# Two loads moved to ScalarE's queue, a read-back moved ahead of x, and two weight conversions regrouped in the start of a fused SSD and PReLU kernel

## The chip, the cores and the metric

The kernel runs on one core of one Trainium2 chip. The metric is the device time of one execution, in microseconds (us); lower is better. One core has a tensor engine (PE, matmuls; PEld is its weight load), VectorE (DVE), ScalarE (ACT), GpSimd (POOL) and SyncE (SP). Loads and stores are issued by SP or ACT into their own queues and carried out by 16 DMA engines.

## The reference

Two blocks follow each other. The first is a state-space scan over 4 batches, 8 heads, 768 tokens, with 32 values of x and 16 values of B and C per head and token, and one decay `a` per head and token. In chunks:

```
y_intra = (C B^T * decay between the two tokens, causal) x
y_inter = (C state) * product of the decays since the chunk began
state   = product of the chunk's decays * state + sum of B x * decays to the chunk's end
```

The second takes the result as 3072 tokens of 256 values and computes `h = x @ w_in` (256 to 2048), `g = max(h, 0) + alpha * min(h, 0)` with one alpha per column, and `out = g @ w_out` (2048 to 256). `w_in` and `w_out` arrive as float64 (8 bytes a value), everything else as float32.

## The kernel before

**Tiles and stages.** A chunk is Q = 128 tokens; two chunks are a pair (`gp`, 12 in all), two pairs are a group of 512 tokens (6 in all). For each pair the kernel loads B, C (into the tile `nat`), x (`xt`) and decays, scans, and writes the result turned into `xT` (`xts[g]`), from which the hidden matmuls read. The first group is special. `first_two` (L821) makes pairs 0 and 1 with decays spread by PE from a short form, in half chunks of 64 tokens; during it the first weights arrive and are converted. After it, group 0 goes through `hidden` and `output` one column block `f` of 128 at a time (loop at L1454), while pairs 2 and 3 are made beside it; from group 1 on `quad` does the weight products.

**Weights.** `w_in` and `w_out` come in eight pieces each (`in_pieces`, `out_pieces`), 512 KB as doubles. Their order in `pieces` (L1413) is in 0, in 1, in 2, out 0, in 3, out 1, in 4, out 2 and so on. `load_weights` (L252) puts one into a tile `raw` (six buffers) through SP. The conversion to float32 has these steps:
- `convert_a` (L262): ACT makes the magnitude of the high word (L273, `wt`); POOL, or DVE where `by` says so, clamps it (L278); ACT makes the low part (L283 or L286, `wg`).
- `sign` (L291): DVE takes the sign bit (L296, `wr`).
- `convert_b` (L300): DVE shifts and xors (L308).
- `convert` (L312): POOL adds both parts into `w_in` or `w_out` (L330).

`convert_next` (L1423) does the last step of the next piece in order, may begin another, and loads one when six are on their way.

**What sets the order.** The order of the instructions on each engine is written out by hand: each engine and each queue runs its instructions in the order in which the program gives them, and waits where data isn't there. So all that follows is read from the text of `first_two`:
- clamps and first scans; `spread` (L858), PE's products that fill the decay banks; `rows_short` (L488), which stores a short form of the products to DRAM (`short`, L500); `rows_out` (L472), a store of `z`;
- `load_pair(1)` (L170): on SP B, C, B, C (L192), x, x (L197); then `load_second` (L228), which reads `short` back, spread over partitions, into the tile `ap` of pair 1 (L231). a of pair 1 (`a1`) has been loaded in `load_pair(0)` by SP (L209, through L133);
- pair 0: `scan` (L870), `turned` (L837, transposes and copies of B and C), `spread_c` (L851), `gram_of` (L874), `added` (L890, the states' increments), `times` (L886), `states` (L903), `mask` (L914, through `one_at_a_time`);
- `first_a` (L539), which clamps `a1` on DVE into `z1`, and the loads of piece 2, of the first half of pair 2 and of piece 3;
- the conversion of piece 0 (L1013, L1014, L1022), around pair 0's `x_products` (L922), `state_products` (L935) and `spread` for pair 1; `copy_out` (L945), four ACT copies into `xT`;
- `hidden_two` (L1102) for columns 0 and 1 of pair 0's tokens; the scans of pair 1 with the conversion of piece 1 between them (L1029 to L1037); pair 1's `turned`, `added`, `states`;
- `rows_products` (L439, a scan on DVE, L441), then on SP the second B and C of pair 2, piece 4, `rows_sent` (L445, its store `pf`), x, piece 5, `abc` (L160, decays spread from `z`), `ap` of pair 2 (L168, which reads `pf` back), `abc`, pieces 6 and 7;
- `hidden_two` for columns 2 and 3, with pair 1's `gram_of`, `times`, last state, `x_products`, `state_products` and `copy_out` placed among its matmuls by `among`; then piece 2 and the rest.

`keep_warm` (L335) puts matmuls without a use where PE would stand.

Of the kernel before, what the change touches and what calls it, by code (L numbers as in the profile page):

```python
# [22 lines left out]
def kernel(  # L23
# [32 lines left out]
    P = 128  # L56
# [113 lines left out]
    def load_pair(gp, decays=True, parted=False):  # L170


        b, c = divmod(2 * gp, CPB)
        turned = gp > GC
        nat = ldx.tile([P, 3, 2, H * N], F32, name="nat")
        xt = ldx.tile([P, 2, HD], F32, name="xt")

        ap = ldx.tile([P, 2 * Q], F32, name="ap")
        if gp == 0:
            load_a(ap, b, c)  # L180
        elif gp > NB:
            load_products(gp, ap)
        if gp == 0:
            load_rows(0, nc.scalar)
        abc = []
        if gp >= HALF:
            load_tokens(nat[:, 0], B[b], c * Q)
        def load_bc(k):
            ts = slice((c + k) * Q, (c + k + 1) * Q)
            for i, src in enumerate((B,) if turned else (B, C)):  # L190
                eng = nc.scalar if gp == 0 and i else nc.sync
                eng.dma_start(out=nat[:, i, k].rearrange("p (h n) -> p h n", h=H),  # L192
                              in_=src[b, :, ts, :].rearrange("h p n -> p h n"))

        def load_x(k):
            ts = slice((c + k) * Q, (c + k + 1) * Q)
            nc.sync.dma_start(out=xt[:, k].rearrange("p (h d) -> p h d", h=H),  # L197
                              in_=x[b, :, ts, :].rearrange("h p d -> p h d"))

        for k in range((1 if parted else 2) if gp < HALF else 0):  # L200
            load_bc(k)
            if gp >= NB:
                load_x(k)
        for k in range(2 if gp < NB else 0):
            load_x(k)
        if gp == 0:
            nc.scalar.dma_start(out=al_n, in_=moe_alpha.rearrange("(k p) -> k p", p=P))
            loads["a", 1] = prep.tile([P, 2 * Q], F32, name="a1")
            load_a(loads["a", 1], b, c + 2)  # L209
        for i, src in enumerate((B, C) if turned else ()):  # L210
# [12 lines left out]
        if decays:  # L223
            for part in load_spread(gp, b, c):
                pass
        return lambda: load_bc(1), lambda: load_x(1)

    def load_second():  # L228

        rows = scratch["short", 0].rearrange("(b h c) t -> b h (c t)", b=2, h=H)  # L230
        nc.sync.dma_start(out=loads["p", 1][3], in_=rows[0, :, 2 * Q : 4 * Q].unsqueeze(1)  # L231
                          .to_broadcast([H, N, 2 * Q]))

    al_n = const.tile([NF, P], F32, name="al_n")
    load_pair(0)
# [22 lines left out]
        raws[id(dst)] = raw  # L258

    parts = {}  # L260

    def convert_a(dst, src, sg, by=nc.gpsimd):  # L262

# [557 lines left out]
    def first_two():  # L821
# [157 lines left out]
        spread(z0, sp)  # L979
        prq = rows_short(rq)  # L980
        rows_out(0)
        load_pair(1)
        load_second()
        nat1, _, xt1, pf1 = loads["p", 1]
        for r in range(4):
            scan(0, r, sp[r])
# [5 lines left out]
        nc.tensor.transpose(al_p[:, :NF], al_n, ident[:NF, :NF])  # L992
        keep_warm(al_p[:, Q:], 1, 3 * Q)
        nc.scalar.copy(out=alpha, in_=al_p[:, :NF])
        bn0 = pair_loads(0)
        slopes(alpha)
        gram_of(bc0, cz0, sp)
# [2 lines left out]
        nc.vector.tensor_tensor_scan(out=pf0, data0=z0.rearrange("p k t -> p (k t)"),  # L1000
                                     data1=starts_a, initial=0.0, op0=ALU.mult, op1=ALU.add)
        cd0 = decayed_c(bc0, pf0)
        for r in (0, 1):
            times(0, r, sp[r])
        states(0, dps, pf0)
        one_at_a_time(0, range(3))
        for r in (2, 3):
            times(0, r, sp[r])
        z1 = first_a(loads["a", 1], nc.vector, lent[1][:, 2:])
        load_next()  # L1010
        load_bc, load_x = load_pair(2, False, True)
        load_next()
        convert_a(*pieces[0], by=nc.vector)  # L1013
        convert_b(*pieces[0], ways=2)  # L1014
        y = places([ss(), ss()], [hp, tp])
        x_products(y, xt0, 0, (0,))
        sp = [bank(r) for r in range(4)]
# [1 line left out]
        x_products(y, xt0, 0, (1,))  # L1019
        state_products(y, 0, cd0)  # L1020
        spread(z1, sp)
        convert_next(halves=(nc.gpsimd, nc.gpsimd))  # L1022
        xts[0] = xtp.tile([P, KC, GT], F32, name="xT")
        copy_out(0, y)
        prelu_of = {0: hidden_two(0, 0, 0, spare())}
        keep_warm(sp[3][:, 2 * Q :], 1)


        scan(1, 0, sp[0])  # L1029
        convert_a(*pieces[1])  # L1030
# [27 lines left out]
        next(spread_loads)  # L1058
        load_next(2)
        keep_warm(second, 1)  # L1060

        def among(i, k):
# [357 lines left out]
            load_weights(*p)  # L1420
        loaded[0] += n

    def convert_next(first=True, **kw):  # L1423


        i = done[0]
        if i < len(pieces):
            convert(*pieces[i], **kw)
# [151 lines left out]
```

## Time and profile before

| | |
|---|---|
| median of 3 runs | 356.28 us (356.27 to 356.45) |
| span of the profiled execution | 355.9 us (355.92) |
| its own whole time | not given by the page; the median less the span is 0.36 us |
| PE busy | 349.3 us, 98% of the span, 2985 matmuls |
| DVE, ACT, POOL busy | 235.8, 171.8, 204.4 us |
| idle time of PE between matmuls | 3.2 us, all before 46 us |
| granted clock of PE | full in all slices |
| DMA | 30.24 MB, 105581 packets, 79896 of them under 512 B |

The profile is that of one execution. Its page gives, for each engine, how long it was busy; a busy PE includes the matmuls that only keep it warm. The timeline lists an engine's instructions in order: start, length, line, operation, output<-inputs, shape, count, and in brackets the idle time before it with what ended it. SPq and ACTq are the issues of loads; their length is the time that the issue held the queue, not the time to landing. The chain of waits goes back from the last instruction to what released it each time. Views by stretch of time give each engine's busy time there, PE's clock, the share in which the DMA engines were busy, and GB/s.

### The profile page before, as it was taken

To read this page: it belongs to the slowest core of one execution; us is meant where nothing else is said; L and a number is where in the kernel's file an instruction comes from. 1 tells how busy PE (TensorE), PEld (TensorE's weight loads), DVE (VectorE), ACT (ScalarE), POOL (GpSimd) and SP (SyncE) were. 2 spreads that over 40 slices of the span, in tenths; PEclk is the share of its full clock that TensorE was granted. 3 is DMA by queue.
4 is the path that set the end of the run, shared out by engine and by line. 5 is a ranking of instruction groups with operands and counts; after the bars stand their busy time and mean duration, and the time that the engine had idled before them with its cause. 6 is when DMAs were issued, how large, how long until landed. Compare 5 with 4: busy or idle time off the path is not lost.

```text
span 355.9 us, 7778 instructions
## 1 busy us (share of the span) xinstructions
PE 349.3 (98%) x2985; PEld 284.4 (80%) x2985; DVE 235.8 (66%) x482; ACT 171.8 (48%) x391; POOL 204.4 (57%) x228
## 2 busy tenths in 40 slices
PE   8899999999999999999999999999999999999996
PEld 4576665578788888888888888888888888888885
DVE  6876986998748756847747856757856633643363
ACT  3477576535355346345345445345445344443431
POOL 6776568589939855725646626637526535434520
PEclk9999999999999999999999999999999999999999
DMA  7899989607345403503423423422001001001102
GB/s 138 182 202 270 329 174 279 148 17 159 106 83 128 102 3 75 104 2 77 78 57 74 86 51 71 85 55 65 11 2 31 0 2 29 2 1 31 31 0 59
DMA packets 105581, 30.24 MB, mean 85 GB/s; under 512 B 79896, under 2 KB 101448, under 8 KB 105544
## 3 DMA queue, kind: packets, MB, share of 16 engines
q1 hardware_dynamic: 103048, 29.43, 36.3%
q10 hardware_dynamic: 2496, 0.32, 0.6%
q8 instruction: 23, 0.38, 0.5%
q14 instruction: 14, 0.11, 0.1%
HBM read 26.32 MB, written 3.42 MB: 84 GB/s over the span
## 4 chain that ended last, share of the span: by engine, by line
PE 89%; SPq 4%; DMA 3%; DVE 2%; ACT 1%; POOL 1%; issue 0%; DVEq 0%; ACTq 0%
PE bank L1216 33%; PE hp L1241 29%; PE bank L1142 6%; PE ss L1241 6%; PE hp L1095 3%; DMA raw<-in_moe_w_in_dram 2%; SPq L192 2%; PE ss L787 1%; PE ss L731 1%; PE hp L1110 1%; PE bank L1209 1%; PE ss L805 1%; PE ss L779 1%; DMA xt<-in_x_dram 1%; SPq L197 1%; PE ss L742 1%
## 5 line engine op out<-in xcount | busy, mean ns | idle before, releaser
L1298 POOL TENSOR_TENSOR gt<-gt 128x512 f32<-128x512 f32 x58 | 74.2, 1279 | 21.1 <-DVE gt L1226 16.3
L1216 PE MATMUL bank<-gt,w_out 128*128 128x256 f32 x320 | 83.5, 381 | 0.0
L1216 PEld LDWEIGHTS bank<-gt,w_out 128*128 128x128 f32 x320 | 60.1, 190 | 9.2 <-issue 1.0
L1288 POOL TENSOR_TENSOR gt<-gt 128x512 f32<-128x512 f32 x20 | 25.4, 1269 | 62.5 <-DVE gt L1226 49.7
L1226 DVE SCALAR_TENSOR_TENSOR gt<-hp,s_mul,gt 128x256 f32<-128x256 f32 x96 | 42.0, 479 | 29.1 <-ACT gt L1224 26.8
L1224 ACT ACTIVATE gt<-hp,s_alpha 128x256 f32<-128x256 f32 x96 | 40.3, 471 | 34.5 <-PE hp L1241 31.4
L1216 PE MATMUL bank<-gt,ws 128*128 128x256 f32 x224 | 55.9, 379 | 0.0
L1216 PEld LDWEIGHTS bank<-gt,ws 128*128 128x128 f32 x224 | 42.3, 190 | 5.6
L1241 PE MATMUL hp<-xs,w_in 128*128 128x256 f32 x160 | 41.9, 384 | 0.0
L1241 PE MATMUL hp<-xs,ws 128*128 128x256 f32 x160 | 41.1, 380 | 0.0
L1267 DVE TENSOR_TENSOR hp<-hp,u 128x512 f32<-128x512 f32 x20 | 14.0, 700 | 35.2 <-ACT u L1265 35.2
L1241 PEld LDWEIGHTS hp<-xs,ws 128*128 128x128 f32 x160 | 30.3, 190 | 4.3 <-POOL xs L1183 0.2
L1241 PEld LDWEIGHTS hp<-xs,w_in 128*128 128x128 f32 x160 | 29.7, 190 | 4.5
L1142 PE MATMUL bank<-w_out,gt 128*128 128x256 f32 x128 | 31.1, 385 | 0.4 <-POOL w_out L330 0.4
L1142 PEld LDWEIGHTS bank<-w_out,gt 128*128 128x128 f32 x128 | 23.6, 190 | 7.2 <-issue 2.9
L1241 PE MATMUL ss<-xT,w_in 128*128 128x256 f32 x96 | 24.6, 379 | 0.0
L645 POOL TENSOR_TENSOR sm<-state,bmask 128x256 f32<-128x256 f32 (+1 forms) x10 | 6.2, 620 | 29.0 <-DVE state L642 29.0
L1095 PE MATMUL hp<-xT,w_in 128*128 128x512 f32 x48 | 22.8, 596 | 0.0
L561 DVE TENSOR_TENSOR_SCAN dec<-abc,bank 128x192 f32<-128x192 f32 x48 | 22.7, 522 | 0.0
L1256 ACT COPY m<-hp 128x512 f32<-128x512 f32 x8 | 4.7, 586 | 35.7 <-PE hp L1241 35.7
L1265 ACT COPY u<-hp 128x512 f32<-128x512 f32 x20 | 11.7, 585 | 19.4 <-PE hp L1241 19.4
L1226 DVE SCALAR_TENSOR_TENSOR gt<-c,s_mul,gt 128x256 f32<-128x256 f32 x40 | 20.6, 555 | 0.0
(232 smaller groups left out, 608.2 us busy)
## 6 DMA issues: line engine op xcount, KB each, us to landing
abc<-z SPq DMA_DIRECT2D x24, 192.0 KB
raw<-in_moe_w_in_dram SPq DMA_DIRECT2D x8, 512.0 KB
raw<-in_moe_w_out_dram SPq DMA_DIRECT2D x8, 512.0 KB
abc<-z SPq DMA_DIRECT2D x8, 512.0 KB
out_dram<-o_sb SPq DMA_DIRECT2D x32, 64.0 KB
nat<-in_B_dram SPq DMA_DIRECT2D x26, 64.0 KB
xt<-in_x_dram SPq DMA_DIRECT2D x12, 128.0 KB
xt<-in_x_dram SPq DMA_DIRECT2D x24, 64.0 KB
```

The source lines that it names most:

```text
L192: eng.dma_start(out=nat[:, i, k].rearrange("p (h n) -> p h n", h=H), in_=src[b, :, ts, :].rearrange("h p n -> p h n"))
L561: nc.vector.tensor_tensor_scan(out=dv[:, o : o + SQ], data0=abc[k][:, s : s + SQ], data1=ident_p[0][:, :SQ], initial=0.0, op0=ALU.mult, op ...
L1095: nc.tensor.matmul(hp, w_in[:, k, f * P : (f + 1) * P], xts[g][:, k], start=(k == 0), stop=(k == KC - 1))
L1142: nc.tensor.matmul(pos[0][t // 2][:, t % 2], gt[:, t * Q : (t + 1) * Q], w_out[:, f], start=(f == 0 and t % 2 == 0), stop=(f == NF - 1), s ...
L1216: nc.tensor.matmul(ms[g][i][:, h], w, blocks[g, z][n][:, p], start=(q == 0 and h == 0), stop=(q == NQ - 1), skip_group_check=True)
L1224: nc.scalar.mul(o[:, p], h[:, p], s_alpha[:, fs[p]])
L1226: nc.vector.scalar_tensor_tensor(out=o[:, p], in0=h[:, p], scalar=s_mul[:, fs[p]], in1=o[:, p], op0=ALU.mult, op1=ALU.max)
L1241: nc.tensor.matmul(to[:, p], w(2 * z + p), b, start=start and p == 0, stop=True, skip_group_check=True)
L1265: nc.scalar.copy(out=u2, in_=A)
L1267: nc.vector.tensor_tensor(out=Y, in0=Y, in1=u2, op=ALU.add)
L1288: nc.gpsimd.tensor_tensor(out=tc_, in0=g22, in1=g12, op=ALU.subtract)
L1298: eng.tensor_tensor(out=o, in0=x0, in1=x1, op=ALU.subtract)
```

## The change

- `load_pair`: for pair 1 C is no longer loaded with B. A new `load_c`, on ACT's queue, loads it; `first_two` calls it twice behind the copy of alpha (L994).
- `a1` is loaded through ACT's queue, behind alpha's load.
- The read-back of `short` into `ap` of pair 1 stands in `load_pair`, after B and ahead of x; `load_second` is gone.
- `first_a` for pair 1 stands ahead of pair 0's first `times`.
- Piece 0 is converted by a new `convert_first`, after `spread` of pair 1: ACT's magnitude and low part by halves, sign whole, DVE's clamp and xor by halves, then `copy_out`, then ACT's second low part, then POOL's two adds.
- Piece 1 is clamped by DVE instead of POOL, and its whole conversion on DVE stands between the first and the second scan of pair 1.
- `rows_products`, its store and the loads behind it stand after the second `hidden_two` with its `among`, ahead of piece 2's second step; the second B and C of pair 2 and piece 4 stay where they were.

```diff
-            for i, src in enumerate((B,) if turned else (B, C)):
+            for i, src in enumerate((B,) if turned or gp == 1 else (B, C)):
...
+        def load_c(k):
+            ts = slice((c + k) * Q, (c + k + 1) * Q)
+            nc.scalar.dma_start(out=nat[:, 1, k].rearrange("p (h n) -> p h n", h=H),
+                                in_=C[b, :, ts, :].rearrange("h p n -> p h n"))
...
+        if gp == 1:
+            rows = scratch["short", 0].rearrange("(b h c) t -> b h (c t)", b=2, h=H)
+            nc.sync.dma_start(out=ap, in_=rows[0, :, 2 * Q : 4 * Q].unsqueeze(1)
+                              .to_broadcast([H, N, 2 * Q]))
         for k in range(2 if gp < NB else 0):
             load_x(k)
...
-            load_a(loads["a", 1], b, c + 2)
+            load_a(loads["a", 1], b, c + 2, nc.scalar)
...
-        return lambda: load_bc(1), lambda: load_x(1)
-
-    def load_second():
...
+        return lambda: load_bc(1), lambda: load_x(1), load_c
...
+    def convert_first(dst, src, sg, copies):
...
+        def magnitude(k):
+            nc.scalar.activation(out=t[:, k].bitcast(F32), in_=hi[:, k].bitcast(F32),
+                                 func=ACTF.Abs, scale=0.125)
+
+        def low(k):
+            nc.scalar.activation(out=g[:, k], in_=half[:, k], func=ACTF.Copy,
+                                 scale=2.0**-11, bias=2.0**25)
+
+        magnitude(0)
+        low(0)
+        magnitude(1)
+        nc.vector.tensor_single_scalar(out=r, in_=hi, scalar=SIGN, op=ALU.bitwise_and)
+        for k in range(2):
+            tk = t[:, k]
+            nc.vector.tensor_scalar(out=tk.bitcast(F32), in0=tk.bitcast(F32), scalar1=F64_INF,
+                                    scalar2=F64_ZERO, op0=ALU.min, op1=ALU.max)
+            nc.vector.scalar_tensor_tensor(out=r[:, k], in0=tk, scalar=3, in1=r[:, k],
+                                           op0=ALU.logical_shift_left, op1=ALU.bitwise_xor)
+        copies()
+        low(1)
+        for k in range(2):
+            nc.gpsimd.tensor_tensor(out=d[:, k], in0=r[:, k], in1=g.bitcast(U32)[:, k], op=ALU.add)
...
-        load_pair(1)
-        load_second()
+        load_c = load_pair(1)[2]
...
         nc.scalar.copy(out=alpha, in_=al_p[:, :NF])
+        for k in range(2):
+            load_c(k)
         bn0 = pair_loads(0)
...
         cd0 = decayed_c(bc0, pf0)
+        z1 = first_a(loads["a", 1], nc.vector, lent[1][:, 2:])
         for r in (0, 1):
             times(0, r, sp[r])
...
-        z1 = first_a(loads["a", 1], nc.vector, lent[1][:, 2:])
...
-        convert_a(*pieces[0], by=nc.vector)
-        convert_b(*pieces[0], ways=2)
...
         spread(z1, sp)
-        convert_next(halves=(nc.gpsimd, nc.gpsimd))
         xts[0] = xtp.tile([P, KC, GT], F32, name="xT")
-        copy_out(0, y)
+        convert_first(*pieces[0], lambda: copy_out(0, y))
+        convert_next(first=False, ready=moe_w_in.dtype != F32)
...
         scan(1, 0, sp[0])
-        convert_a(*pieces[1])
-        sign(*pieces[1])
-        scan(1, 1, sp[1])
+        convert_a(*pieces[1], by=nc.vector)
         convert_b(*pieces[1])
-        for r in (2, 3):
+        for r in (1, 2, 3):
             scan(1, r, sp[r])
...
-        rpf = rows_products()
         load_bc()
         load_next()
-        rows_sent(rpf)
-        load_x()
-        load_next()
-        spread_loads = load_spread(2, *divmod(4, CPB))
-        next(spread_loads)
-        load_products(NB, loads["p", NB][3])
-        next(spread_loads)
-        load_next(2)
         keep_warm(second, 1)
...
         prelu_of[2] = hidden_two(0, 2, 0, second, among)
+        rows_sent(rows_products())
+        load_x()
+        load_next()
+        spread_loads = load_spread(2, *divmod(4, CPB))
+        next(spread_loads)
+        load_products(NB, loads["p", NB][3])
+        next(spread_loads)
+        load_next(2)
```

With `ready=True`, `convert_next` only counts the piece as done and doesn't convert it.

More of the change, by code (lines that the diff above doesn't have):

```diff
@@ L225, in load_pair @@
                 pass
-        return lambda: load_bc(1), lambda: load_x(1)
-    def load_second():
-        rows = scratch["short", 0].rearrange("(b h c) t -> b h (c t)", b=2, h=H)
-        nc.sync.dma_start(out=loads["p", 1][3], in_=rows[0, :, 2 * Q : 4 * Q].unsqueeze(1)
-                          .to_broadcast([H, N, 2 * Q]))
+        return lambda: load_bc(1), lambda: load_x(1), load_c
     al_n = const.tile([NF, P], F32, name="al_n")
@@ L260 @@
     parts = {}
+    def convert_first(dst, src, sg, copies):
+        if src.dtype == F32:
+            copies()
+            return
+        d = dst.bitcast(U32)
+        raw = raws.pop(id(dst))
+        hi = raw[:, :, :, 1]
+        half = raw.rearrange("p k w t -> p k (w t)").bitcast(U16)
+        half = half.rearrange("p k (w t) -> p k w t", t=4)[:, :, :, 1]
+        t = wtp.tile([P, 2, WQ], U32, name="wt")
+        g = wtp.tile([P, 2, WQ], F32, name="wg")
+        r = wtp.tile([P, 2, WQ], U32, name="wr")
+        def magnitude(k):
[14 more added lines that the diff above has]
+                                           op0=ALU.logical_shift_left, op1=ALU.bitwise_xor)
+        copies()
+        low(1)
+        for k in range(2):
+            nc.gpsimd.tensor_tensor(out=d[:, k], in0=r[:, k], in1=g.bitcast(U32)[:, k], op=ALU.add)
     def convert_a(dst, src, sg, by=nc.gpsimd):
@@ L1008, in first_two @@
             times(0, r, sp[r])
-        z1 = first_a(loads["a", 1], nc.vector, lent[1][:, 2:])
         load_next()
-        load_bc, load_x = load_pair(2, False, True)
+        load_bc, load_x, _ = load_pair(2, False, True)
         load_next()
-        convert_a(*pieces[0], by=nc.vector)
-        convert_b(*pieces[0], ways=2)
         y = places([ss(), ss()], [hp, tp])
@@ L1421, in load_next, with convert_next @@
         loaded[0] += n
-    def convert_next(first=True, **kw):
+    def convert_next(first=True, ready=False, **kw):
         i = done[0]
         if i < len(pieces):
-            convert(*pieces[i], **kw)
+            if not ready:
+                convert(*pieces[i], **kw)
             if first and i and i + 2 < len(pieces):
```

## The prediction

> **What bounds the kernel now.** I read the page first: PE is busy for 349.3 of the 355.9 us and holds 89% of the chain of work that ended last, so time can be won only where PE stands still. The chain of waits over the first 60 us shows where that is: everything before 46 us is the start, and after it the chain is PE alone.
>
> ```profile
> 9.40 3.52 SPq L192
> ...
> 29.84 7.45 DMA raw<-in_moe_w_in_dram
> ...
> 40.34 2.33 DVE dec L567 x4
> ...
> 44.52 1.28 POOL w_out L330
> ...
> 45.84 1.99 PE bank L1142 x8
> ```
>
> Columns: start, length, what. A DMA issue that SP could not finish for 3.52 us; a weight piece that took 7.45 us from issue to landing; DVE's scans; POOL's last step of a w_out piece; then output(4) on PE. Behind that line no stall of PE over 0.03 us follows, so a shift of the start survives to the end only if the work released at 45.84 shifts too. Second, PE's timeline with its idle times (the other gaps: 0.53 at 8.27, 0.27 at 21.81):
>
> ```profile
> 14.11 2.04 PE L1110 MATMUL hp<-xT,w_in 128*128 128x256 f32 x8 [0.85 <-POOL w_in L330]
> ...
> 17.54 0.35 PE L895 MATMUL ss<-xt,bn 64*32 64x64 f32 x16 [0.25 <-DMA xt<-in_x_dram]
> ...
> 45.84 0.48 PE L1142 MATMUL bank<-w_out,gt 128*128 128x256 f32 x1 [0.44 <-POOL w_out L330]
> ```
>
> The first hidden matmuls wait for the converted first piece, `added` waits for x of pair 1, output(4) for out_pieces[2]. Third, DVE around pair 1:
>
> ```profile
> 18.30 0.98 DVE L910 SCALAR_TENSOR_TENSOR gt<-gt,ap,ss 128x64 f32<-128x64 f32 x3 [0.72 <-DMA ap<-short]
> 19.20 0.83 DVE L441 TENSOR_TENSOR_SCAN rpf<-r,zeros 96x128 f32<-96x128 f32 x1
> 20.08 1.42 DVE L887 TENSOR_TENSOR dec<-bank,dec 128x256 f32<-128x256 f32 x4
> ```
>
> `states` waits for the products `ap`, then `rows_products` (0.83 us) stands between it and `times`, which x_products on PE needs. Fourth, SP's queue, and the DMA engines (last two columns: busy share, GB/s):
>
> ```profile
> 9.40 3.52 SPq L192 DMA_DIRECT2D nat<-in_B_dram  x1
> 12.96 0.58 SPq L192 DMA_DIRECT2D nat<-in_C_dram  x1
> 13.59 1.21 SPq L197 DMA_DIRECT2D xt<-in_x_dram  x2
> 14.84 0.67 SPq L231 DMA_DIRECT2D ap<-short  x1
> ```
> ```profile
> 12.00:13.50 1.50, 1.25 (x44) 0.94 (x42) 1.22 (x4) 1.50 (x7) 0.22 (x1) 1.00 0.24 28
> ...
> 38.00:42.00 4.00, 4.00 (x27) 2.30 (x26) 3.50 (x7) 4.00 (x9) 2.71 (x3) 1.00 1.05 403
> ```
>
> SP hangs in B's second issue until 12.92 while the DMA engines run dry (share 0.24); from 30 to 42 they are full (0.99 to 1.05).
>
> **The change, part by part.** All starts are those of the profile before.
>
> *a of pair 1 on ScalarE's queue.* SP loses 0.65 + 0.05 us, so the weights are issued at 5.10, not 5.80. ACT gains one issue of 0.65 to 0.80 (rows L133): its table load (1.28, at 3.69) ends at 5.77 at the latest, and its first copy starts at 5.79, so it is hidden with 0.02 to spare; past that, bc, cz and alpha (8.11) follow one for one. The bytes still go through the same engines (share 0.87 from 6 to 8), beside x and B of pair 0. Landing of the first piece (11.54): between 0.7 earlier and 0.3 later; I take 0 to 0.2 earlier, since the engines were nearly full.
>
> *C of pair 1 on ScalarE's queue.* Two issues behind the alpha copy (ends 8.28). Nearest row: ACT's own C issues, 1.30 for two; ACT is taken until 9.6, and its next work is the L906 copy at 9.51: cost 0 to 0.1, covered by PE's two warm matmuls (10.14 to 11.27). Queued behind: L906, then the first piece's conversion.
>
> *z1 earlier on DVE.* 0.28 + 0.06, into the 0.40 that DVE waits for L881 before `times` (8.97). Free if a1 has landed by 8.6; it was not waited for at 11.26, so its landing isn't bounded by a row here; taken as free.
>
> *First piece by halves.* Now ACT L273 0.67, L283 0.66, then four copies, DVE clamp 0.43 and two 0.38, POOL two 0.85; PE at 14.11. Half-size ACT steps: bounds 0.37 (L847 copy) and 0.57 (half of L286 x2); I take 0.42 (L1120, also 128x256). From 11.54: magnitudes and low part end at 11.96, 12.31, 12.66; DVE clamps a half in 0.28 (L437, 128x252) and xors in 0.38: 12.62 and 13.36; POOL follows 0.16 later (23.60 to 23.76): first half ready at 13.63, 0.48 earlier. The second half waits for ACT: copies to 13.40, low(1) to 13.78, POOL to 14.75, against 14.97. So the four matmul pairs end 0.2 to 0.5 earlier; I take 0.35. With 0.57 per ACT step it is 0.
>
> *Second piece.* Its clamp leaves POOL (0.61 at 15.05) for DVE (0.43), ahead of scans 1 to 3 (1.9 together); the 0.72 that DVE waited for that clamp goes. Scans end near 17.35 instead of 17.57, POOL's bn1 and the piece itself come 0.9 earlier.
>
> *Products ahead of x, no C between.* On SP: short and z stores, B, B, then `ap`, which reads back the short store, x, x, next weight piece. B's second issue no longer stalls behind a full queue, but SP now waits for the short store to land. The trace's landing events put that at 13.05 (the last of its completions). Then `ap` 0.1 + 0.67, x from 13.86 (13.59 before), the next piece from 15.1 (15.55). x now meets empty engines instead of C's 1024 packets of 64 B, so it lands at 16.6 to 17.7 against 17.50; I take 17.1. `ap` lands near 15.5 against 18.2, and L910's 0.72 wait goes; next late are the scans.
>
> *rows_products moved.* Times start when L881 is done (19.2) instead of 20.08; x_products ends 1.1 earlier, and with 0.2 of issue left over PE enters the L1110 run at 22.3 instead of 23.2: **0.9 ahead**. Its new place is after L296 (22.81): 0.83 more before L308 and POOL's 1.40 of piece 2 (ends 25.16, needed 27.28): hidden by 2.1 - 0.83. Its store waited for nothing at 24.15 on SP; with the scan done at 23.64 at the latest there is 0.5 of cover. Without it, pf, `ap` of pair 2 (which already waits 0.9 for pf) and all weights behind slip one for one. x, out_pieces[1], two abc, `ap` and two more pieces move with it, in the same SP order.
>
> *What is late next.* PE comes to output(4) 0.9 sooner, but that needs in_pieces[4] landed (37.29) and, from there to 45.8, DVE without a pause over 0.5. Those landings follow SP's stream through full engines. The stream gains between 0 (same bytes) and 1.1 us (1.5 us at share 0.24 refilled); the read-back of short leaves 0.45 at the next weight piece, and I take 0.5 to 0.6. PE's wait at 45.84 then grows from 0.44 to about 0.8 and swallows the rest.
>
> The Trainium skill (DMA: Bandwidth & Descriptors, Issuing engines are not separate DMA queues) says that loads started by different engines share the same 16 DMA engines, so that only issue time is saved. The trace agrees: 3178 packets in 1.5 us with two queues (2119 per us), 1096 in 0.5 us with one (2192). By the rule alone the stream gains 1.9 us of issue at most; by the rows the engines are the limit and it gains the 0.5.
>
> **Sum.** Span 355.92 - 0.55 = 355.37. The page gives no whole time; the median 356.28 stands 0.36 above the span, taken as unchanged: **355.7**.
>
> **Rivals.**
> 1. *The stream gains its 1.1 us or more.* For it: share 0.24 and the 3.52 us. Against: the wait for short. Then PE's 0.9 and most of the 0.44 count: 1.0 to 1.4, so 354.9 to 355.3.
> 2. *Hidden anyway.* Landings at 32.5 and 37.3 unchanged, because the engines are full; PE is early and waits 1.3 at 45.84, or the halves gain nothing since the second still ends near 14.97. Time 356.1 to 356.5.
> 3. *Slower: ScalarE is held by its own loads.* At 37.30 SP waited 0.7 for a weight piece that this load of B or C doesn't touch; the trace has it waiting on the completion semaphore that the weight load of 29.84 also posts to. So a load can wait for an earlier one whose semaphore it takes over. If a C load draws that of the first piece (11.52), ACT stands from 8.3 to past 11.5, L906 slips from 9.51 to 12.2, and with it states, masks and state_products: +2.6, less 0.9 of gains: 358.0. It decides as soon as that predecessor lands after 9.5. Against: earlier loads that landed by 8.7 can as well come first in turn.
>
> **Chances.** Forecast (355.3 to 356.1) 0.47, rival 1 0.25, rival 2 0.13, rival 3 0.15. About 0.2% (0.7 us) is what a measurement here tells from no change: faster means under 355.57. That is rival 1 and a quarter of the forecast: 0.37; slower is rival 3, 0.15; the rest 0.48. Range 354.9 to 357.0: the forecast, rivals 1 and 2 and a slip of 0.7; most of rival 3 lies above it, and some 0.03 below.
>
> **What would show it.** Right: L1110's first wait 0.85 falls under 0.5; L910 no longer waits for `ap`; L1110's second run starts near 22.3; the landing for L273 at 37.3 comes near 36.7, and PE still waits before L1142 near 45.3, by 0.5 to 1.0. Wrong: ACT idle from 8.3 to 11.5 or later (rival 3), that landing unmoved (2), or no PE wait there at all (1). A chance difference in which DMA engine lags would make me wrong without any of these steps.

## The result and the profile after

| | median of the runs | range |
|---|---|---|
| before | 356.32 us (6 runs) | 355.95 to 358.01 |
| after | 362.34 us (6 runs) | 361.03 to 363.73 |

The ratio is 1.0161, 95% interval 1.0135 to 1.0186: the change makes the kernel slower by 6 us. The forecast of 355.7 and its range to 357.0 were wrong; rival 3 named what happened, at 358.0. The profiled execution took 361.64 us with a span of 359.9. The six times after lie in two groups, 361.03 to 361.64 and 363.04 to 363.73, with the median between them; the profiled one is of the lower group, and what parts the two wasn't found.

In the changed kernel lines stand lower: the states' copy L906 is now L946, `states` on DVE L950, `times` L927, x_products L969, the spread L905, `added` L935, first hidden matmuls L1146, warm matmuls L378; C of pair 1 is L197, the last step of the first piece L300.

ScalarE's timeline (start, length, engine, line, what; in brackets the idle time before it and its releaser):

```profile
8.06 0.17 ACT L1033 COPY alpha<-ss 128x16 f32<-128x16 f32 x1
12.09 1.40 ACTq L197 DMA_DIRECT2D nat<-in_C_dram  x2
13.53 0.21 ACT L946 COPY gt<-hp 128x64 f32<-128x64 f32 x1 [5.30 <-DMA nat<-in_B_dram]
```

The same stretch in the kernel before:

```profile
8.11 0.17 ACT L994 COPY alpha<-ss 128x16 f32<-128x16 f32 x1
9.51 0.21 ACT L906 COPY gt<-hp 128x64 f32<-128x64 f32 x1 [1.23 <-PE hp L895]
```

The copy of alpha ends at 8.23. The next thing in ScalarE's program is the first C load, and its issue starts only at 12.09; the second ends at 13.49, and L946, which had started at 9.51 in the kernel before (as L906), comes at 13.53. The releaser named is a load of B, whose data L946 doesn't read. The landing events show what ScalarE waited for. The loads and stores of SyncE and ScalarE take eight completion semaphores (numbers 100 and 102 to 108 in the trace) in turn. The turn is that of the compiled program, and neither that of the text nor that of the issue times: numbers 105 to 108 go next to the second B of pair 2 (issued at 15.61), the first C (12.09), the second C of pair 2 (16.12) and the second C of pair 1 (13.05). So the first C load takes over that of the store of `z`, whose last completion is at 12.07, the second that of the second B of pair 1, at 13.03; the issues start 0.02 us behind each (12.09 and 13.05).

VectorE and GpSimd wait for L946, and PE for VectorE. PE's timeline:

```profile
15.17 0.89 PE L969 MATMUL hp<-dec,xt 64*32 64x64 f32 x32 [3.96 <-DVE dec L927]
...
18.55 3.12 PE L1146 MATMUL hp<-xT,w_in 128*128 128x256 f32 x8
...
28.13 2.21 PE L1146 MATMUL hp<-xT,w_in 128*128 128x256 f32 x9
```

The second half of x_products starts 3.96 us late, the first hidden matmuls at 18.55 instead of 14.11, and the eight of them take 3.12 us instead of 2.04. Why they are longer stands in the view by stretches (stretch, length, PE busy with its matmuls, granted clock, DMA share, GB/s):

```profile
12.00:15.00 3.00, 0.00 (x0) 0.84 0.50 83
15.00:18.00 3.00, 2.83 (x68) 0.50 1.17 241
18.00:22.00 4.00, 4.00 (x35) 0.64 1.06 199
```

The same stretches in the kernel before:

```profile
12.00:15.00 3.00, 2.15 (x48) 1.00 0.59 61
15.00:18.00 3.00, 2.75 (x45) 1.00 0.96 209
18.00:22.00 4.00, 3.73 (x101) 1.00 0.84 150
```

Behind the idle time PE's clock is half, where before it was full. From x_products' second half to the end of the hidden matmuls PE takes 6.33 us (15.17 to 21.50) instead of 4.79 (11.20 to 15.99), and 0.85 of the 4.79 was the wait for the first piece, which is gone here: the same work went from 3.94 us to 6.33. The prediction's sum of rival 3 had no term for this. Of the span's 4.0 us more than in the execution profiled before, 2.4 are idle time of PE (5.62 against 3.20) and the rest is PE being slower.

From the second run of hidden matmuls on (columns 2 and 3, 28.13 here), nothing differs any more: the span ends 331.8 us after its start. In all thirteen profiled executions of this study that distance is 331.7 to 331.9 us, except in three where PE also waits 0.44 us for w_out before output(4); there it is 332.7 to 332.9, which is 1.0 more, of which that wait explains 0.44. So a version's worth can be read at one row, to about 1 us: when that run starts.

### The profile page after: what moved, and what is told of

Same layout as the page of the kernel before. It is cut to its first block, busy times and chain, and to the rows that moved or that the text cites. A ratio compares the mean times of both kernels' runs of the same rounds, so it can differ in the third digit from the quotient of the medians.

```text
span 359.9 us, 7780 instructions
## 1 busy us (share of the span) xinstructions
PE 350.8 (97%) x2985; PEld 286.1 (79%) x2985; DVE 237.9 (66%) x484; ACT 172.4 (48%) x393; POOL 203.3 (56%) x227
## 4 chain that ended last, share of the span: by engine, by line
PE 95%; DMA 1%; ACTq 1%; ACT 1%; DVE 0%; issue 0%; POOL 0%; SPq 0%
PE bank L1252 33%; PE hp L1277 28%; PE bank L1178 8%; PE hp L1131 6%; PE ss L1277 6%; PE hp L1146 2%; DMA nat<-in_B_dram 1%; PE ss L827 1%; PE ss L771 1%; PE bank L1245 1%; PE ss L845 1%; PE ss L819 1%; PE ss L782 1%; PE ss L981 1%; PE ss L658 1%; PE bank L1146 0%
## 5 line engine op out<-in xcount | busy, mean ns | idle before, releaser
L1277 PE MATMUL hp<-xT,ws 128*128 128x256 f32 x80 | 20.5, 379 | 0.0
```

Of the source, the lines that this page charges most:

```text
L1277: nc.tensor.matmul(to[:, p], w(2 * z + p), b, start=start and p == 0, stop=True, skip_group_check=True)
```

## The experiments

Theory H: ScalarE is held, because each C load waits for the landing of the load or store whose completion semaphore it takes over. Theory K: on top of it PE's clock, lowered by the idle time, costs about as much as the difference that is left. The rival was that other parts of the change (conversion, order of loads, `rows_products`) are slower in themselves. The first hidden matmuls are L1144 instead of L1146 in c_on_sp, loads_back and pe_longer, and L1110 in the kernel before.

| run | first hidden matmul | second run | span | median us | ratio (95%) |
|---|---|---|---|---|---|
| before, as predicted from | 14.11 | 23.20 | 355.9 | 356.28 | |
| before, once more | 13.65 | 22.18 | 353.9 | 356.26 | 0.9999 (0.9988 to 1.001) |
| after | 18.55 | 28.13 | 359.9 | 362.34 | 1.0161 (1.0135 to 1.0186) |
| c_on_sp | 13.79 | 23.41 | 355.2 | 357.13 | 1.002 (1.0003 to 1.0036) |
| c_alone | 20.43 | 30.19 | 362.0 | 363.79 | 1.0205 (1.0181 to 1.0228) |
| warm | 17.67 | 26.77 | 358.5 | 360.57 | 1.0114 (1.009 to 1.0138) |
| c_pool | 14.75 | 24.62 | 356.5 | 356.64 | 1.001 (0.9992 to 1.0028) |
| c_before_b | 14.02 | 23.04 | 354.8 | 356.64 | 1.0014 (1.0 to 1.0027) |
| loads_back | 14.67 | 23.02 | 354.8 | 356.54 | 1.0009 (0.9998 to 1.0021) |
| conv_only | 14.28 | 22.84 | 355.7 | 356.41 | 0.9999 (0.9986 to 1.0012) |
| pe_longer | 14.30 | 23.11 | 356.0 | 356.42 | 0.9995 (0.9972 to 1.0018) |
| c_early_a_sp | 14.34 | 23.27 | 355.0 | 356.97 | 1.0004 (0.9987 to 1.002) |
| c_early_z_late | 14.16 | 23.05 | 354.8 | 356.51 | 0.9997 (0.9987 to 1.0008) |

The first four columns are of one profiled execution each, median and ratio of all runs of a kernel, against the runs of before on the same chip. An execution's whole time is its span plus 1.67 to 1.78 us. So the profiles of before (some 357.6 by this), c_pool (358.28), pe_longer (357.76) and conv_only (357.43) are of executions 1.0 us or more slower than the median of their kernel.

**c_on_sp.** C of pair 1 back on SyncE's queue, everything else as changed.

```diff
-            for i, src in enumerate((B,) if turned or gp == 1 else (B, C)):
+            for i, src in enumerate((B,) if turned else (B, C)):
...
-        for k in range(2):
-            load_c(k)
```

> The changed kernel, except that C of pair 1 is loaded by SP again, right behind each B (B, C, B, C, then the read-back, x, x). Theory H (ScalarE is held): in the changed profile ACT does nothing between the alpha copy (ends 8.23) and the L946 copy (13.53), and its two C issues start at 12.09 and 13.05, within 0.05 us of the last landing of the z store (12.07) and of the second B of pair 1 (13.03), whose completion semaphores they take over. Without those loads on ACT the L946 copy is back near 9.5, PE's idle time of 3.96 us before x_products goes, and the time falls from 362.3 to 355.3 to 356.3. Rival D (the DMA order, that is the read-back that holds SP and the early a, costs the time): it stays at 360 or above.

The loss is all but gone: 357.13, over the 355.3 to 356.3 expected and still 0.2% (0.7 us) slower than before. L946 waits for PE and not for a load, on ScalarE's timeline:

```profile
9.95 0.21 ACT L946 COPY gt<-hp 128x64 f32<-128x64 f32 x1 [1.23 <-PE hp L935]
```

What is left is not a gain. The first hidden matmuls start at 13.79, but PE then waits for x of pair 1, which lands at 17.95 behind the read-back of `short`, C and B:

```profile
18.00 0.35 PE L935 MATMUL ss<-xt,bn 64*32 64x64 f32 x16 [0.82 <-DMA xt<-in_x_dram]
```

**c_alone.** The kernel before, with nothing but C of pair 1 moved to ScalarE's queue, at the same place.

```diff
-            for i, src in enumerate((B,) if turned else (B, C)):
+            for i, src in enumerate((B,) if turned or gp == 1 else (B, C)):
...
         nc.scalar.copy(out=alpha, in_=al_p[:, :NF])
+        for k in range(2):
+            load_c(k)
```

> The kernel before, with one part of the change alone: C of pair 1 on ScalarE's queue behind the alpha copy. In this program's order the first C load takes over the completion semaphore of the first B of pair 1, the second that of the first x of pair 1. Theory H: ACT stands until those have landed (near 13 and 16 us), so the L946 copy, 9.51 before, comes at 15.5 to 17.5, and the time is 6 to 9 us above the kernel before, more than the whole change costs: 362 to 365. Rival I (only the two issues, 1.3 us, and the shared DMA engines cost): at most 357.6.

363.79: the one edit costs more alone than the whole change. The semaphores that the two loads take over are now those of the first B and the first x of pair 1; these landed at 13.60 and 14.97, and the issues start at 13.62 and 15.00. ScalarE's timeline (the states' copy is L911 here):

```profile
13.62 1.75 ACTq L197 DMA_DIRECT2D nat<-in_C_dram  x2
15.41 0.21 ACT L911 COPY gt<-hp 128x64 f32<-128x64 f32 x1 [6.91 <-DMA xt<-in_x_dram]
```

PE stands 5.56 us before x_products' second half, at 17.05. So the other edits aren't needed for the loss; H decides, and which load stands eight back in the turn sets the size.

**warm.** The changed kernel with five warm matmuls instead of one ahead of x_products' second half, so that PE has work, without a use, in the idle time.

```diff
-        keep_warm(sp[0], 1, GT)
+        keep_warm(sp[0], 5, GT)
```

> The changed kernel with five warming matmul pairs instead of one ahead of the second half of pair 0's x_products, so that PE works through most of the 3.96 us for which it waits. In the changed profile PE's clock is granted below full in the slices from 9 to 27 us and the eight hidden matmuls of L1146 take 3.12 us instead of 2.04. Theory K (some 1.5 us of the loss is this clock, from 15.17 to 21.50 against 11.20 to 15.99 before): the time falls by 1.0 to 2.0 us, to 360.3 to 361.3. Rival (the loss is the wait alone, the clock's part is made good later): 361.8 to 362.8.

360.57, 1.8 us below the changed kernel. ScalarE is held in the same way: its two issues start at 12.44 and 13.42, behind landings at 12.42 and 13.40, and L946 comes at 13.92. But the clock is 1.00 in all three stretches that showed 0.84, 0.50 and 0.64:

```profile
12.00:15.00 3.00, 3.00 (x8) 1.00 0.41 63
15.00:18.00 3.00, 2.82 (x79) 1.00 1.16 223
18.00:22.00 4.00, 3.85 (x48) 1.00 1.05 231
```

That is theory K. Its price by the medians is rough, as the four times (360.26 to 360.84) are of another chip and the intervals of the two ratios just touch. Within an execution it is the same: from L946 to the second run of hidden matmuls it takes 14.60 us in the changed kernel (13.53 to 28.13), 12.85 here (13.92 to 26.77) and 12.73 in the kernel before, once more (9.45 to 22.18). The 4.0 us by which L946 is late (13.53 less 9.51) and this 1.8 make 5.8 of the 6.0 us.

The Trainium skill (TensorE: Matmul & The Clock Gate, Part 1: The HAM clock gate) says that TensorE goes back to half of its clock when it has stood idle for a window of about 3.4 us. The row agrees: 3.96 us of idle time, then 0.50. It doesn't cover the profiled execution of c_pool below, where a stretch at 0.52 followed a single idle time of 1.32 us.

**c_pool.** C of pair 1 on GpSimd's queue, which takes other semaphores.

```diff
-            nc.scalar.dma_start(out=nat[:, 1, k].rearrange("p (h n) -> p h n", h=H),
+            nc.gpsimd.dma_start(out=nat[:, 1, k].rearrange("p (h n) -> p h n", h=H),
...
-        for k in range(2):
-            load_c(k)
         bn0 = pair_loads(0)
+        for k in range(2):
+            load_c(k)
```

> The changed kernel, with C of pair 1 loaded through GpSimd's queue, between pair 0's first product (L573) and the slopes; GpSimd's loads have completion semaphores of their own. Theory H: ACT isn't held, L946 starts near 9.5, and the time is 355.0 to 356.5, with GpSimd busy for some time with the two issues, which can delay masks and with them PE by up to 0.7. Rival D: 360 or above, as any queue other than SP puts C's packets beside the weights.

356.64, just over the 355.0 to 356.5 expected: ScalarE isn't held (L946 at 9.53), the issue of both loads takes GpSimd 2.03 us. No gain over the kernel before either. The lowered clock is that of the profiled execution and not of the version: its mean is 0.994, where the eleven others have 0.998 or more. It happens in the kernel before too: of its 23 executions on this chip two have a mean of 0.995, and took 358.38 and 359.10 us, the others at most 357.11.

**c_before_b.** The sharpest test of H: C stays on ScalarE, but so early in the order that the loads eight back have landed when ScalarE comes to it.

```diff
+        _ = [load_c(k) for k in range(2 if gp == 1 else 0)]
         for k in range((1 if parted else 2) if gp < HALF else 0):
             load_bc(k)
...
-        for k in range(2):
-            load_c(k)
```

> The changed kernel, but ScalarE issues both C loads of pair 1 right behind a1, ahead of its table load. The order in which loads take over the eight completion semaphores then gives them the predecessors C and B of pair 0, whose landings end at 4.81 and 5.33 in the profile of the changed kernel. Theory H (a load is held until the load whose semaphore it takes over has landed): both issues pass without a hold, by about 6 us; ScalarE pays only the issues, 0.8 to 1.3 us ahead of the table load, so the copy of prt starts at 7.1 to 7.6 instead of 6.29, the states' copy L946 at 10.0 to 11.0 instead of 13.53, and the time is 356.5 to 358.5. Rival (ScalarE's queue is slow or full for loads of C, whatever the semaphores): the issues take ScalarE past 8 us again, L946 stands past 12 and the time is 361 or more.

ScalarE's timeline:

```profile
4.97 1.01 ACTq L197 DMA_DIRECT2D nat<-in_C_dram  x2
6.01 1.28 ACT L551 ACT_TABLE_LOAD   x1 [6.01 <-DMA nat<-in_B_dram]
...
10.18 0.21 ACT L946 COPY gt<-hp 128x64 f32<-128x64 f32 x1 [1.23 <-PE hp L935]
```

The same two loads on the same queue take 1.01 us, and the time is 356.64. Their semaphores are those of the first C and the first B of pair 0, which had landed at 4.79 and 5.32; the issues start 0.18 and 0.06 later, at 4.97 and 5.38. The margin is small: in c_early_a_sp below, which comes to them sooner, the second issue starts at 4.83, 0.03 behind its predecessor's landing, and the two take 1.47. So neither ScalarE's queue nor C is at fault; the cost is in when the load eight back lands. The bracket of the table load shows a trap: ScalarE was issuing loads all the time before it, and an idle time that ends with such a row isn't one.

**loads_back** and **conv_only.** What are the rest worth? The first undoes all three load moves and keeps the conversions, `z1` and `rows_products`; the second is the kernel before with the conversion edits alone.

```diff
 loads_back, against the changed kernel, beside the edit of c_on_sp
+        for k in range(2 if gp < NB else 0):
+            load_x(k)
         if gp == 1:
             rows = scratch["short", 0].rearrange("(b h c) t -> b h (c t)", b=2, h=H)
...
-            load_a(loads["a", 1], b, c + 2, nc.scalar)
+            load_a(loads["a", 1], b, c + 2)
 conv_only, against the kernel before
-        convert_a(*pieces[0], by=nc.vector)
-        convert_b(*pieces[0], ways=2)
...
-        convert_next(halves=(nc.gpsimd, nc.gpsimd))
...
-        copy_out(0, y)
+        convert_first(*pieces[0], lambda: copy_out(0, y))
+        convert_next(first=False, ready=moe_w_in.dtype != F32)
...
-        convert_a(*pieces[1])
-        sign(*pieces[1])
-        scan(1, 1, sp[1])
+        convert_a(*pieces[1], by=nc.vector)
         convert_b(*pieces[1])
-        for r in (2, 3):
+        for r in (1, 2, 3):
```

> The changed kernel with all three load moves undone: a1 and C of pair 1 by SyncE, the read-back of the products behind x. What stays are the halves of the first piece, the second piece's clamp on VectorE, z1 earlier and rows_products later. If these four are worth what the prediction gave the halves and the scans together, the time is 355.6 to 356.1 beside 356.3 before. If x of pair 1 and the landings of the weights take the gain away, it is 356.2 to 356.6, and the wait of PE at output(4) is back with 0.4 us or more. If rows_products in its new place holds back its store and the weights behind it, it is 356.7 or more.

> The kernel before with only the conversion edits: the first piece by halves, the second clamped by VectorE ahead of the scans. All loads, z1 and rows_products stand as before. By the prediction's 0.35 us for the halves, with PE's wait at output(4) swallowing part of it: 355.9 to 356.3, and the first hidden matmuls at 13.7 to 13.9 instead of 14.11. If the landings at 37 us are the limit, 356.2 to 356.4, with a longer wait at output(4).

356.54 and 356.41, both no different from before. The wait for output(4) that loads_back was expected to show isn't there. The expected reasons failed in part: in both the first hidden matmuls start late, 14.67 and 14.28, though the first half is ready at 13.16 and 13.38. In loads_back the weight load of the first of them (PEld) stands alone for 1.27 us:

```profile
13.22 0.19 PEld L1144 LDWEIGHTS hp<-xT,w_in 128*128 128x128 f32 x1 [0.25 <-POOL w_in L300]
14.67 0.40 PEld L1144 LDWEIGHTS hp<-xT,w_in 128*128 128x128 f32 x2 [1.27 <-issue]
```

The matmul of that weight load also starts at 14.67, and carries no wait on a semaphore. It is the same place in PE's program in all these kernels (449 instructions recorded before it). A packet of 16 KB, of a queue that the trace calls one of instructions, lands shortly before: at 13.10 here, 12.84 in conv_only and 12.97 in c_pool, which has such a stall too (weight load 13.84, matmul 14.75). In before, before_again, c_on_sp and c_before_b it lands at 12.12 to 12.55, and the matmul follows its weight load within 0.11 us. Theory F: the packet holds PE's next instructions, and PE stands at the border of a block that has not come. The trace doesn't name PE as the queue's owner; that rests on this tie.

**pe_longer.** loads_back with a few more instructions on PE for the same work.

```diff
-        keep_warm(sp[0], 1, GT)
+        keep_warm(sp[0], 2, GT // 2)
```

> In the two kernels with the halves and the loads of before, PE's weight load for the first hidden matmul starts 0.05 us after GpSimd's first half is done (13.22 and 13.44), and the matmul itself only at 14.67 and 14.28; that matmul carries no wait on a semaphore. In both a 16 KB packet of PE's own instruction queue lands at 13.10 and 12.84, later than in the kernels where that matmul follows its weight load at once (12.11 to 12.55). This kernel is the one with all three load moves undone, with the warm matmul L1057 of 512 columns written as two of 256: the same work, a few more instructions ahead of the hidden matmuls. Theory F (PE stands at the border of an instruction block that isn't there yet): the border now falls some instructions earlier, so if the packet lands at 12.8 or later, the idle time of 0.5 to 1.5 us shows among the matmuls of the second spread (L905), and the first hidden matmul follows its weight load within 0.15 us. Rival (something about the first hidden matmul itself, its operands or its bank): the idle time stays between that weight load and that matmul. Time 356.0 to 357.0 by both.

PE's timeline:

```profile
12.69 0.69 PE L905 MATMUL bank<-gt,ident 32*64 32x128 f32 x31
14.06 0.32 PE L905 MATMUL bank<-gt,ident 32*64 32x128 f32 x1 [0.69 <-issue]
14.30 0.92 PE L1144 MATMUL hp<-xT,w_in 128*128 128x256 f32 x3
```

The idle time has moved, with the border, in front of the last matmul of the spread, and the hidden matmuls follow without a gap. The stall again has 449 recorded instructions of PE ahead of it. Theory F's forecast of the place holds, though the packet landed at 12.61, a little under the 12.8 that I had set for it; the stall ends 1.45 us behind the packet (1.57, 1.44 and 1.78 in the other three).

**before_again.** The kernel before, unchanged.

> The kernel before, profiled once more. In the five profiled executions seen of other kernels here the whole time stands 1.67 to 1.78 us above the span. If that holds for this kernel too, the 0.36 us that the prediction took as lying around the span is an artefact of setting one execution's span against the median of others: time minus span 1.7, and for a time near 356.3 a span near 354.6. If this kernel is different: 0.4, with a span of 355.9.

It took 355.65 with a span of 353.9: 1.75 between them. So the execution that the prediction read, with its span of 355.9, was one of some 357.6 us and not of the median. Its first piece landed at 11.52; here at 10.15, and the hidden matmuls wait less:

```profile
13.65 0.64 PE L1110 MATMUL hp<-xT,w_in 128*128 128x256 f32 x2 [0.46 <-POOL w_in L330]
```

**c_early_a_sp** and **c_early_z_late.** Two attempts at a version that beats both: C on ScalarE early as in c_before_b, a1 back on SyncE; then `z1` back in its old place as well.

```diff
 c_early_a_sp, against c_before_b
-            load_a(loads["a", 1], b, c + 2, nc.scalar)
+            load_a(loads["a", 1], b, c + 2)
 c_early_z_late, against c_early_a_sp
-        z1 = first_a(loads["a", 1], nc.vector, lent[1][:, 2:])
         for r in (0, 1):
             times(0, r, sp[r])
...
             times(0, r, sp[r])
+        z1 = first_a(loads["a", 1], nc.vector, lent[1][:, 2:])
         load_next()
```

> An attempt at a version that beats both. ScalarE issues both C loads of pair 1 ahead of its table load, as in the run before (357.92 to 356.45, median 356.64), but a1 is issued by SyncE again, as in the kernel before. The 1.20 us of a1's issue then no longer stand ahead of the table load, which starts near 4.8 instead of 6.01, and the copy of prt near 6.1 instead of 7.30, so gram_of on PE starts at 8.2 to 8.4 instead of 8.94. If the start of the chain is what the other one lacked: 355.6 to 356.2. If the first weight piece, the first landings or PE's instruction packet set the first hidden matmuls anyway: 356.3 to 356.7. If ScalarE is held again by a completion semaphore: L946 past 12 and 361 or more.

> The run before (ScalarE issues C of pair 1 ahead of its table load, a1 by SyncE; median 356.97) with one more part undone: first_a for pair 1, which makes z1, stands behind pair 0's second times again, as in the kernel before. In the run before, VectorE waited 1.72 us for a1 in that place, until 9.79, and PE 0.95 us for times at 10.47. If that wait is what the version lacks, PE's idle time ahead of x_products falls under 0.3 us, the first hidden matmuls start at 13.6 to 14.0 instead of 14.34, and the time is 356.0 to 356.6. If PE's instruction packet (landed 12.42) and x of pair 1 set the time in any case, 356.7 to 357.1.

The first missed, at 356.97. gram_of did come earlier (8.31), but VectorE then stood for a1, ahead of `times`:

```profile
9.79 0.29 DVE L477 TENSOR_SCALAR gt<-a 128x252 f32<-128x252 f32 x1 [1.72 <-DMA a<-in_a_dram]
```

PE lost 0.95 us to that at 10.47. The second took this wait away and came to 356.51, inside its first band, though the hidden matmuls at 14.16 didn't reach the 13.6 to 14.0 that belonged to it: gram_of came at 8.80, as PE's 32 matmuls of the spread at 4.5 us had taken 1.16 us, against 0.70 in c_early_a_sp and in the changed kernel, and the second transposes behind them began 0.6 later. Why PE is slower there in some executions wasn't found. Neither is faster than before. No version that I ran is.

## Why the prediction was wrong

The step that failed is "C of pair 1 on ScalarE's queue": "cost 0 to 0.1, covered by PE's two warm matmuls". It priced the two issues by their length, 1.30, and took it that they would start when ScalarE was free. They started when the semaphores were free, at 12.09 and 13.05, which made L946 4.0 us late, left PE idle for 3.96 and halved its clock behind that. Undoing it removes the loss (c_on_sp), doing it alone makes a loss of the same kind (c_alone), and placing it behind loads that have landed makes it harmless (c_before_b).

- **Rival 3** had the mechanism, place and condition ("as soon as that predecessor lands after 9.5"), but got 0.15, on the ground that loads landed by 8.7 could as well come first in turn. Which load stands eight back doesn't have to be left to chance: the compiled program gives it before any run, and c_alone's two predecessors were named rightly in that way. It can't be counted off the text. Its price was short three times: the predecessors landed at 12.07 and 13.03, not at 11.52 (2.6 became 4.0); the 0.9 of gains taken off did not come; and the clock, 1.8, was missing.
- **a1 on ScalarE's queue**, "0.65 to 0.80, hidden with 0.02 to spare": the issue took 1.20 (3.77 to 4.97), the table load ended at 6.28 instead of 5.77 at the latest and the copy of prt started at 6.29 instead of 5.79. So this term was mis-sized, but it cost PE nothing that can be seen: with the same 6.29 gram_of starts at 8.22 in the changed kernel (8.27 before), since bc waits for PE's transposes anyway. In c_on_sp gram_of is 0.44 late (8.71), but there PE itself was slow at the start (the spread's 32 matmuls took 1.16 us against 0.70, as in c_early_z_late), and bc waits for it:

```profile
7.21 0.65 ACT L887 COPY bc<-hp 128x256 f32<-128x256 f32 x2 [0.66 <-PE hp L883]
```

  Only in c_before_b, where the two C issues also stand ahead of the table load and prt is copied at 7.30, is gram_of late (8.94) by ScalarE.
- **z1 earlier**, taken as free if a1 has landed by 8.6: right with a1 on ScalarE (8.74 in c_before_b, no wait) and in loads_back with a1 on SyncE (8.44); 0.95 us of PE's time in c_early_a_sp, where a1 came later.
- **First piece by halves.** The 0.42 for ACT's steps and 0.28 for the clamp are right (0.41 to 0.47 and 0.28 to 0.29). The xor of 0.38 is 0.43 for the first half but 0.92 for the second, while GpSimd adds the first half, as VectorE's and GpSimd's rows in loads_back show:

```profile
11.87 0.43 DVE L295 SCALAR_TENSOR_TENSOR wr<-wt,wr 128x256 uint32<-128x256 uint32 x1
...
12.53 0.92 DVE L295 SCALAR_TENSOR_TENSOR wr<-wt,wr 128x256 uint32<-128x256 uint32 x1
```
```profile
12.44 0.73 POOL L300 TENSOR_TENSOR w_in<-wr,wg 128x256 uint32<-128x256 uint32 x1 [1.33 <-DVE wr L295]
```

  The first half is ready 0.37 earlier than in before_again (13.16 against 13.53, with first pieces landing at 10.53 and 10.15), against the 0.48 predicted. The 0.35 by which the four matmul pairs should end earlier came to nothing: in the kernels without the hold, c_pool with its lowered clock apart, PE's next work behind the first eight starts at 15.87 (c_on_sp) to 16.39 (loads_back), against 15.99 and 15.42 in the two executions of before. PE then stands at the block border of theory F, or waits for x. The Trainium skill (SBUF — State Buffer, Who interferes with whom) says that VectorE and GpSimd contend for one shared port pair, and that it is an exclusive lock. The rows fit that: GpSimd's add ends at 13.17, and the xor, begun at 12.53, only at 13.45. No run here takes the two apart.
- **Second piece.** The clamp on VectorE took 0.86 in c_before_b, c_on_sp and conv_only and 0.41 in loads_back, where 0.43 was assumed, and the scans ended at 17.8 to 18.6, not at 17.35. Before, they had ended at 17.57 and 16.89.
- **Products ahead of x.** The landing of the `short` store was the right thing to wait for: it landed at 11.88 in the changed kernel and 12.90 in c_before_b, and `ap` was issued 0.07 and 0.06 behind it. x landed at 17.35 and 17.39 (17.1 was taken), and in c_before_b the waits for `ap` and x are gone; in c_on_sp x came at 17.95. The "full queue" of the 3.52 us is not shown: B's second issue took 0.67 in the changed kernel, and what held it before stays open. The hold of this document wasn't it, as the semaphores had been free since 8.14.
- **rows_products moved**: its own cost can't be told, since in loads_back with it the second run starts at 23.02 and in conv_only without it at 22.84, both after delays of their own. In the changed kernel its store left SyncE at 28.35 (24.15 before), with SyncE idle from 22.66, so the loads behind it came 4.2 us late as well; PE waited for none of them. What the term left out: `times` of pair 1 also needs gram_of, which ended at 20.03 before, 0.05 ahead of `times` at 20.08. With the scan moved, VectorE waits for PE there instead: 0.66 in c_before_b, 0.73 in loads_back, 1.12 in c_on_sp. The 0.9 could come only with an earlier gram_of.
- **What is late next**: "PE still waits before L1142 by 0.5 to 1.0". Not in the changed kernel. The wait of 0.44 is there in three of the thirteen profiles, and the one I read was among them. So the landings at 37 us aren't a steady limit; the start of the second run is.
- **The offset of 0.36** was the median of some executions less the span of another; within one it is 1.67 to 1.78 in every run. This didn't shift the forecast, as the gain was in effect taken from the median, but it hid that the waits being priced (0.85 for the first piece, 0.44 at output(4)) belonged to an execution slower than most.

What stays open: why a gain of 0.3 to 0.4 us in the first half never reaches the second run of hidden matmuls. Its start lies between 22.84 and 23.41 in all kernels without the hold, except for c_pool with its slowed clock, while before gave 22.18 and 23.20 in two executions. x of pair 1, the block border, a1, gram_of ahead of `times` and a slow start of PE were each seen as the late one, but no run removed them all.

## What to carry to other kernels

Before a load is moved to a queue whose engine also computes, read in the compiled program, or in a trace, which completion semaphore it takes over and from which load (here the one eight back in a turn that SyncE's and ScalarE's queues share, and that isn't the order of the text): the engine stands, with all that is queued behind, until that load has landed. If that landing is late, put the load further forward in the order, not on another engine alone, or on a queue with semaphores of its own (GpSimd's in c_pool). And add to a stall of several us on PE what its lowered clock costs afterwards, here nearly half as much again (1.8 on 4.0).

## What the runs showed of the hardware

- The issue of a load on ScalarE started 0.02 us behind the last completion on the semaphore that it took over (12.07 to 12.09 and 13.03 to 13.05 after, 12.42 to 12.44 and 13.40 to 13.42 in warm), and 0.02 to 0.03 in c_alone (13.60 to 13.62, 14.97 to 15.00); with predecessors landed 0.18 and 0.06 us before, the two issues took 1.01 us (c_before_b).
- Behind 3.96 us of idle time PE's granted clock was 0.50 for at least 3 us; it was also 0.52 behind an idle time of 1.32 us (c_pool), but full behind one of 1.46 us (loads_back). What decides in the short cases wasn't found.
- Packets of 16 KB of an instruction queue are in the trace among those of the data; four executions show PE standing 0.7 to 1.5 us behind the same count of its instructions (449 recorded) until 1.4 to 1.8 us after such a packet landed, and with four more instructions ahead of the hidden matmuls the stall came four instructions sooner in the work (pe_longer). That these are PE's instructions is inferred.
- The broadcast load of a1 took ScalarE 1.19 to 1.24 us to issue, while SyncE issued x beside it, and SyncE 0.64 to 0.75; why isn't shown.
